# Spreading the last gates of an input phase over the first steps of the output phase, in a fused attention and expert kernel

## Chip, cores and metric

The kernel runs on one core of one Trainium2 chip. The metric is the device time of one execution in microseconds. Engines are named as in the profile: PE is TensorE (PEld its weight loads), DVE is VectorE, ACT is ScalarE, POOL is GpSimd, SP the queue that issues the DMAs.

## What is computed

The reference cut to its core: an attention with a local and a global window, then two expert layers on 3072 tokens.

```python
x = attention(q, k, v)                   # 3072 x 512 after the heads are joined
a, b = x @ w1, x @ w2                    # 512 -> 1024
x2 = ((a * b) @ w3) @ w_out              # first layer, 1024 -> 1024 -> 512
h = x2 @ w_in                            # second layer, 512 -> 2048
g = h * np.cos(h)                        # the gate
out = g @ w_out2                         # 2048 -> 512
```

## The kernel before

Float32 matmuls run as three passes over values that are split into a high half (a cast to fp32r) and a low half (value minus high half): high x high, high x low, low x high (`mm3`, line 419). So every activation that goes into TensorE needs a cast on ScalarE and a subtraction on VectorE ahead of it. A step's first matmul needs only the high half of its activation, the second the low half.

Attention and the first expert layer end at about 615 us of the span. The stage behind it is the second layer, which the change touches. It does its two matrix products by a scheme of seven products in place of eight, with sums and differences of quarter blocks formed before and after. The tokens come in three groups q of two times 512. For each q there are two phases:

- **Input phase A** (`phase_a(q, k, ...)`, k = 0 to 7): one round k makes seven products of six matmuls of 512 columns (`prod`) into PSUM banks; VectorE adds them into two pairs of tiles, jj (gate `g0[k]`) and gg, named gr in the profile (gate `g1[k]`), each 128 x 1024. A gate then computes h times cos(h): `turns` on ScalarE (line 1090, an integer tile in PSUM), two argument operations on VectorE (`rest_steps`, line 1099, which read that PSUM tile), `size` and `cosine` on ScalarE (lines 1105 and 1108) and the product `times` (line 1113) on GpSimd. The gates of round k are finished during rounds k + 1 and k + 2; `fold` (line 1236) then takes a difference of two gated blocks, in A on GpSimd.
- **Output phase B** (`phase_b(q)`): 56 steps in the order of the list `turn`. Step `at` takes block (i, k) of product i and does six matmuls. The first 14 steps are blocks (0, 0) to (0, 6) and (3, 0) to (3, 6), then (2, 0) to (2, 6), then the three blocks with k = 7, then four products of eight blocks. `op_split` makes the two halves of a block into a tile "op": a cast on ScalarE (line 1218) and a subtraction on VectorE (line 1219). It runs four steps ahead of its step. The first four (low halves 0 to 3 in what follows) are made in or right behind the last rounds of A, two of them on GpSimd.

When A ends, gates are left over: the product of `g0[6]`, and all of `g1[7]` and `g0[7]` but one `turns`. `last_gates` is a generator that issues them; a `yield` in it ends what one step of B issues. In the kernel before it issues them in three blocks, at steps 0, 1 and 3, ahead of the split of the same step, with the products on GpSimd.

The order of work on each engine is the order in which the code is written (`manual_schedule`): an engine takes its instructions in that order and waits at one whose operands are not there. Tiles come from rings. "op" tiles alternate between two buffers of their own and four of the tag "Wb", by the counter `op_count` modulo 6; the arguments r of the gates take the same four "Wb" buffers, those of the last two gates take two buffers "x2f", into which later the inputs of the next group (`x2_loads`, `x2_steps`) go. `x2_steps` is also a generator: 18 pieces of work on ScalarE and VectorE that prepare the activations of the next group; a part runs in B, the rest in round 0 of the next A. `pieces_to` issues the weight loads on SP's queue ahead of their use. `evict` takes finished PSUM banks out in B.

```python
for i, (l_hi, l_lo, r_hi, r_lo) in enumerate(terms):
    for e, (l, r) in enumerate(((l_hi, r_hi), (l_hi, r_lo), (l_lo, r_hi))):
        nc.tensor.matmul(ps, lhsT=l, rhs=r, ...)
```

Of the kernel before, what the change touches and what calls it, by code (L numbers as in the profile page):

```python
# [13 lines left out]
ALU = mybir.AluOpType  # L14
# [23 lines left out]
NP = M2 // 2  # L38
# [233 lines left out]
def fused(ctx, tc, a_qk, a_v, a_v0, w3p, wo1p, w1p, w2p, winp, wo2p, out):  # L272
    nc = tc.nc
# [476 lines left out]
    with tc.manual_schedule():  # L750
# [234 lines left out]
        def some(steps, n):  # L985
            for _ in range(n):
                next(steps, None)
# [95 lines left out]
        class Gate:  # L1083
# [25 lines left out]
                    self.r, self.r, ACTF.Sin, scale=-1.0, bias=half_pi[:, 0:1]  # L1109
                )  # L1110

            def times(self):
                nc.gpsimd.tensor_tensor(out=self.h, in0=self.r, in1=self.h, op=ALU.mult)  # L1113

        turn = []
        for prods, ks in (
# [24 lines left out]
        g0, g1 = {}, {}  # L1141

        def phase_a(q, k, x2_last):

            pieces_to(2 * q * (NP * 7 // 2) + (7 * k + 13) // 2)
            jj = wts.tile([128, 2, TB2], F32, tag="wB", name="jj")
            gg = p2.tile([128, 2, TB2], F32, tag="gr", name="gr", bufs=8)
            g0[k], g1[k] = Gate(jj), Gate(gg)
            sv = misc.tile([128, 2, TB2], F32, tag="raw", name="sv", bufs=3)
            vv = misc.tile([128, 2, TB2], F32, tag="raw", name="vv", bufs=3)  # L1150
            s1, s, v = sv[:, 0, :], sv[:, 1, :], vv[:, 0, :]

            def add(out, p, q):
                nc.vector.tensor_tensor(out=out, in0=p, in1=q, op=ALU.add)

            def gate(g, at, what, *args):
                if at >= 0:
                    getattr(g[at], what)(*args)

            prod(q, k, 0)  # L1160
            prod(q, k, 1)
            gate(g1, k - 1, "rest")
            gate(g0, k - 2, "cosine")
            nc.scalar.copy(out=s1, in_=banks["a"])
            gate(g0, k - 2, "times")
            gate(g0, k - 1, "turns")
            add(s, banks["b"], s1)
            gate(g1, k - 1, "size")
            gate(g1, k - 1, "cosine")
            gate(g1, k - 1, "times")  # L1170
            if k:
                fold(3, k - 1, nc.gpsimd)
            if k > 1:
                fold(2, k - 2, nc.gpsimd)
            if k >= NP - 2:
                op_split(0, k - NP + 2, nc.gpsimd)
            prod(q, k, 2)
            prod(q, k, 3)
            some(x2_last, 2)
            add(v, banks["c"], s)  # L1180
            if k:
                steps = g0[k - 1].rest_steps()
                next(steps)
            add(gg[:, 1, :], banks["d"], v)
            if k:
                next(steps)
            some(x2_last, 2)
            prod(q, k, 4)
            prod(q, k, 5)
            run(x2_last)  # L1190
            prod(q, k, 6)
            nc.scalar.copy(out=jj[:, 0, :], in_=banks["a"])
            gate(g0, k - 1, "size")
            add(gg[:, 0, :], banks["c"], s)
            g1[k].turns()
            add(jj[:, 1, :], banks["d"], s)
            if k == NP - 1:
                op_split(0, 2)
                op_split(0, 3)

        t3 = {}

# [7 lines left out]
        ops, op_count = {}, [0]  # L1210
# [27 lines left out]
        def last_gates():  # L1238

            k = NP - 1  # L1240
            homes = [
                late.tile([128, 2, TB2], F32, tag="x2f", name="r", bufs=2) for _ in range(2)
            ]
            a, b = g1[k].rest_steps(homes[0]), g0[k].rest_steps(homes[1])
            next(a)
            next(a)
            g0[k - 1].cosine()
            g0[k - 1].times()
            yield
            g0[k].turns()  # L1250
            g1[k].size()
            g1[k].cosine()
            g1[k].times()
            yield
            yield
            next(b)
            next(b)
            g0[k].size()
            g0[k].cosine()
            g0[k].times()  # L1260
            yield

        def phase_b(q):

            final = q == NQ - 1
# [3 lines left out]
            x2_next = None  # L1269
# [66 lines left out]

            for at, (n, k) in enumerate(turn):
                pieces_to(base + pairs_of.index((n, k // 2)) + 6)
                some(gates, 1)
                if at + 4 < len(turn):  # L1340
                    op_split(*turn[at + 4])
                if at in (8, 10, 12):
                    fold(*{8: (2, NP - 2), 10: (3, NP - 1), 12: (2, NP - 1)}[at])
                if at == 8 and not final:
                    x2_loads(q + 1)
                    r0, r1 = (
                        late.tile([128, 2, TB2], F32, tag="x2f", name="x2f", bufs=2)
                        for _ in range(2)
                    )
                    nc.sync.dma_start(out=r0, in_=x2_cols("B12", q + 1))  # L1350
                    x2_next = x2_steps(r0, r1)
                for i, lag in ((1, 21), (6, 31)):
                    if 0 <= at - lag < NP:
                        fold(i, at - lag)
                if x2_next and at >= 16 and at % 3 == 0:
                    some(x2_next, 1)
                if q == 0 and at in (34, 38, 42):
                    flags_of[0] = next(steps_f)
# [106 lines left out]
```

## Time and profile before

| | us |
|---|---|
| median of 3 runs (lowest to highest) | 1122.69 (1121.36 to 1123.53) |
| the profiled execution, its own time | 1121.77 |
| its span in the trace | 1120.0 |
| TensorE busy | 1085.7 |
| VectorE busy | 848.0 |
| ScalarE busy | 730.7 |
| GpSimd busy | 251.2 |
| second expert layer, first to last matmul | 615.35 to 1114.1 |

A window row gives the stretch, its length, then for each engine the busy time and the number of instructions, the granted TensorE clock (1.00 is 2.4 GHz, 0.50 is 1.2 GHz), the share of the DMA engines and GB/s. A timeline row gives the start, the duration, engine, line, operation, output and inputs, and in brackets how long the engine had been idle and what ended that. A row of waits gives who waited for whom, the total, how often and the longest. Busy TensorE is not TensorE at its peak: at half the clock it is busy for twice as long with the same matmuls.

### The profile page before, as it was taken

How to read it: one execution, taken by the hardware profiler on the slowest of the kernel's cores; microseconds unless marked ns; L12 is line 12 of the kernel's file. 1: busy time of each engine (PE TensorE's matmuls, PEld its weight loads, DVE VectorE, ACT ScalarE, POOL GpSimd, SP SyncE). 2: the span in 40 equal slices, each digit the busy share in tenths (PEclk: the TensorE clock that was granted, in tenths of full speed). 3: DMA queues.
4: the chain of work that ended last, by engine and by line, in shares of the span. 5: the costliest groups of instructions: out<-in, count | busy, mean ns of one | idle time of the engine just before them, and what ended most of it. 6: DMA issues, size and time to landing. Idle time of an engine off the chain costs nothing.

```text
span 1120.0 us, 17799 instructions
## 1 busy us (share of the span) xinstructions
PE 1085.7 (97%) x5922; PEld 936.3 (84%) x5922; DVE 848.0 (76%) x1815; ACT 730.7 (65%) x1481; POOL 251.2 (22%) x252
## 2 busy tenths in 40 slices
PE   8999999999999999999999999899999799999897
PEld 5547899999999999999999887587887588887686
DVE  8887677878787876878633688688788697887684
ACT  8988767767767766767523677454578454678452
POOL 0000011111111111111100377100377100377100
PEclk9999999999999999999999999799999899999899
DMA  9854456676667656665360655466655565655362
GB/s 333 284 185 163 153 191 207 208 224 200 220 201 233 210 184 222 212 221 192 114 220 22 216 195 179 168 210 222 225 189 187 171 219 220 233 190 182 105 222 97
DMA packets 88308, 219.24 MB, mean 196 GB/s; under 512 B 9488, under 2 KB 26384, under 8 KB 88208
## 3 DMA queue, kind: packets, MB, share of 16 engines
q1 hardware_dynamic: 87696, 217.44, 58.1%
q8 instruction: 49, 0.80, 0.3%
q10 hardware_dynamic: 512, 0.58, 0.2%
q14 instruction: 51, 0.42, 0.1%
HBM read 176.04 MB, written 41.94 MB: 195 GB/s over the span
## 4 chain that ended last, share of the span: by engine, by line
PE 50%; DVE 7%; ACT 2%; issue 1%; POOL 0%; DVEq 0%; POOLq 0%
PE h_ps L419 29%; PE mm L419 12%; PE k_ps L419 6%; DVE op L1219 3%; DVE r L1099 1%; PE x_ps L644 1%; DVE jj L1236 1%; ACT r L1105 1%; ACT op L1218 1%; PE pt_ps L617 0%; DVE res L1278 0%; ACT r L1108 0%; PE s_ps L559 0%; PE s_ps L555 0%; PE pt_ps L619 0%
## 5 line engine op out<-in xcount | busy, mean ns | idle before, releaser
L610 POOL TENSOR_SCALAR e<-e,st 128x232 f32<-128x232 f32 x148 | 76.1, 525 | 477.0 <-DVE st L602 386.5
L419 PE MATMUL h_ps<-op,piece 128*128 128x512 f32 x576 | 148.8, 416 | 21.7 <-DVE op L1219 13.2
L419 PEld LDWEIGHTS h_ps<-op,piece 128*128 128x128 f32 x576 | 115.0, 202 | 53.6 <-DVE op L1219 16.3
L419 PE MATMUL mm<-xT,wA 128*128 128x384 f32 x768 | 146.8, 340 | 0.5 <-ACT xT L658 0.4
L419 PE MATMUL mm<-ab,W 128*128 128x384 f32 x768 | 146.2, 340 | 0.0
L419 PE MATMUL mm<-xT,wB 128*128 128x384 f32 x768 | 146.2, 339 | 0.0
L419 PE MATMUL h_ps<-T,piece 128*128 128x512 f32 x576 | 138.4, 389 | 0.0
L419 PEld LDWEIGHTS mm<-xT,wA 128*128 128x128 f32 x768 | 130.9, 188 | 3.2 <-issue 1.8
L419 PEld LDWEIGHTS mm<-ab,W 128*128 128x128 f32 x768 | 131.1, 188 | 2.4 <-issue 2.4
L419 PEld LDWEIGHTS mm<-xT,wB 128*128 128x128 f32 x768 | 130.9, 188 | 2.1 <-issue 2.1
L419 PEld LDWEIGHTS h_ps<-T,piece 128*128 128x128 f32 x576 | 108.1, 188 | 22.5
L1113 POOL TENSOR_TENSOR gr<-r,gr 128x1024 f32<-128x1024 f32 x24 | 57.5, 2397 | 285.1 <-ACT r L1108 283.6
L419 PE MATMUL h_ps<-B,piece 128*128 128x512 f32 x432 | 106.3, 390 | 0.7 <-DVE B L948 0.7
L419 PE MATMUL k_ps<-op,piece 128*128 128x512 f32 x432 | 100.5, 390 | 1.2 <-DVE op L1219 1.2
L419 PEld LDWEIGHTS k_ps<-op,piece 128*128 128x128 f32 x432 | 80.8, 188 | 18.9 <-DVE op L1219 2.0
L419 PEld LDWEIGHTS h_ps<-B,piece 128*128 128x128 f32 x432 | 80.9, 188 | 18.1 <-DVE B L948 1.5
L589 ACT ACTIVATE e<-e,top 128x232 f32<-128x232 f32 (+1 forms) x192 | 89.3, 467 | 2.1 <-DVE top L578 2.1
L522 ACT CAST hh<-qk 128x720 fp32r<-128x720 f32 x74 | 58.9, 796 | 46.0 <-PE s_ps L559 42.0
L578 DVE CUSTOM_DVE_ANT_0 e<-s_ps,bias 128x232 f32<-128x232 f32 (+1 forms) x192 | 64.9, 374 | 13.6 <-PE s_ps L559 8.1
L1105 ACT ACTIVATE r<-r 128x1024 f32<-128x1024 f32 x48 | 51.0, 1062 | 35.1 <-DVE r L1099 35.1
L1218 ACT CAST op<-gr 128x512 fp32r<-128x512 f32 x72 | 44.0, 623 | 43.4 <-PE k_ps L419 15.0
L1219 DVE TENSOR_TENSOR op<-jj,op 128x512 fp32r<-128x512 f32 x66 | 54.6, 849 | 17.5 <-ACT op L1218 17.5
(136 smaller groups left out, 1992.0 us busy)
## 6 DMA issues: line engine op xcount, KB each, us to landing
piece<-a_s SPq DMA_DIRECT2D x84, 512.0 KB, 3.3
piece<-o2s SPq DMA_DIRECT2D x84, 512.0 KB, 4.1
qk<-in_a_qk SPq DMA_DIRECT2D x74, 360.0 KB, 3.3
a_s<-ap SPq DMA_DIRECT2D x56, 256.0 KB, 2.4
o2s<-ap SPq DMA_DIRECT2D x56, 256.0 KB, 2.4
v<-in_a_v SPq DMA_DIRECT2D x95, 128.0 KB, 3.3
raw<-in_w3p SPq DMA_DIRECT2D x16, 512.0 KB, 4.9
raw<-in_winp SPq DMA_DIRECT2D x16, 512.0 KB, 3.6
```

Source lines behind the costliest of these rows:

```text
L419: nc.tensor.matmul(ps, lhsT=l, rhs=r, start=first and i + e == 0, stop=last and i == n - 1 and e == 2, skip_group_check=more,)
L522: nc.scalar.copy(out=hh[n], in_=qk_raw[n])
L578: nc.vector.tensor_tensor_reduce(out=es[n][:, e, :w], in0=sp[:, e, :w], in1=bias[:, 2 * p + e, :], scale=-0.125, scalar=3.0e38, op0=ALU.ad ...
L589: nc.scalar.activation(es[n][:, e, :w], es[n][:, e, :w], ACTF.Exp, bias=top[:, n, e:e + 1], scale=-1.0, accum_out=sts[n][:, 0, e:e + 1],)
L610: nc.gpsimd.tensor_scalar(x, x, st[:, 1, e:e + 1], 1.0, ALU.mult, ALU.mult)
L644: nc.tensor.matmul(x[e * 64:(e + 1) * 64, i * 128:(i + 1) * 128], lhsT=vt[:kk, c, e * 64:(e + 1) * 64], rhs=pt[:kk, e, c, :], start=c == 0 ...
L1099: nc.vector.scalar_tensor_tensor(out=self.r, in0=self.kt, scalar=-c, in1=x, op0=ALU.mult, op1=ALU.add)
L1105: nc.scalar.activation(self.r, self.r, ACTF.Abs)
L1113: nc.gpsimd.tensor_tensor(out=self.h, in0=self.r, in1=self.h, op=ALU.mult)
L1218: nc.scalar.copy(out=t[:, 0, :], in_=x)
L1219: engine.tensor_tensor(out=t[:, 1, :], in0=x, in1=t[:, 0, :].bitcast(F32), op=ALU.subtract)
L1236: engine.tensor_tensor(out=out, in0=p, in1=q, op=ALU.subtract)
```

## The change

`times` takes an engine. In the last round of A, GpSimd makes the low halves of steps 2 and 3 and does so ahead of its two folds; the halves of steps 0 and 1 are made one round earlier (rounds 5 and 6). The counter of the op ring is set to zero at the start of each A. `last_gates` is written in 13 pieces instead of four, its three products go to VectorE, and the three last folds on VectorE are part of it. In B a step now issues its split first and its piece of the gates after it. The loads of the next group's inputs go from step 8 to step 14, and their preparation from every third step from 18 on to every second step from 28 on. Two series of folds in B shift by one step.

```diff
--- before.py
+++ after.py
@@ -1109,8 +1109,8 @@
                     self.r, self.r, ACTF.Sin, scale=-1.0, bias=half_pi[:, 0:1]
                 )
 
-            def times(self):
-                nc.gpsimd.tensor_tensor(out=self.h, in0=self.r, in1=self.h, op=ALU.mult)
+            def times(self, engine=nc.gpsimd):
+                engine.tensor_tensor(out=self.h, in0=self.r, in1=self.h, op=ALU.mult)
 
         turn = []
         for prods, ks in (
@@ -1168,12 +1168,17 @@
             gate(g1, k - 1, "size")
             gate(g1, k - 1, "cosine")
             gate(g1, k - 1, "times")
+            if k == NP - 1:
+                op_split(0, 2, nc.gpsimd)
+                op_split(0, 3, nc.gpsimd)
             if k:
                 fold(3, k - 1, nc.gpsimd)
             if k > 1:
                 fold(2, k - 2, nc.gpsimd)
-            if k >= NP - 2:
-                op_split(0, k - NP + 2, nc.gpsimd)
+            if k == 0:
+                op_count[0] = 0
+            if NP - 3 <= k < NP - 1:
+                op_split(0, k - NP + 3, nc.gpsimd)
             prod(q, k, 2)
             prod(q, k, 3)
             some(x2_last, 2)
@@ -1194,9 +1199,6 @@
             add(gg[:, 0, :], banks["c"], s)
             g1[k].turns()
             add(jj[:, 1, :], banks["d"], s)
-            if k == NP - 1:
-                op_split(0, 2)
-                op_split(0, 3)
 
         t3 = {}
 
@@ -1242,22 +1244,34 @@
                 late.tile([128, 2, TB2], F32, tag="x2f", name="r", bufs=2) for _ in range(2)
             ]
             a, b = g1[k].rest_steps(homes[0]), g0[k].rest_steps(homes[1])
+            g0[k - 1].cosine()
+            g0[k - 1].times(nc.vector)
+            g0[k].turns()
             next(a)
+            yield
             next(a)
-            g0[k - 1].cosine()
-            g0[k - 1].times()
-            yield
-            g0[k].turns()
+            yield
+            yield
             g1[k].size()
             g1[k].cosine()
-            g1[k].times()
-            yield
-            yield
             next(b)
+            yield
             next(b)
+            yield
             g0[k].size()
             g0[k].cosine()
-            g0[k].times()
+            g1[k].times(nc.vector)
+            yield
+            yield
+            yield
+            g0[k].times(nc.vector)
+            yield
+            yield
+            fold(2, k - 1)
+            yield
+            fold(3, k)
+            yield
+            fold(2, k)
             yield
 
         def phase_b(q):
@@ -1336,12 +1350,10 @@
 
             for at, (n, k) in enumerate(turn):
                 pieces_to(base + pairs_of.index((n, k // 2)) + 6)
-                some(gates, 1)
                 if at + 4 < len(turn):
                     op_split(*turn[at + 4])
-                if at in (8, 10, 12):
-                    fold(*{8: (2, NP - 2), 10: (3, NP - 1), 12: (2, NP - 1)}[at])
-                if at == 8 and not final:
+                some(gates, 1)
+                if at == 14 and not final:
                     x2_loads(q + 1)
                     r0, r1 = (
                         late.tile([128, 2, TB2], F32, tag="x2f", name="x2f", bufs=2)
@@ -1349,10 +1361,10 @@
                     )
                     nc.sync.dma_start(out=r0, in_=x2_cols("B12", q + 1))
                     x2_next = x2_steps(r0, r1)
-                for i, lag in ((1, 21), (6, 31)):
+                for i, lag in ((1, 20), (6, 32)):
                     if 0 <= at - lag < NP:
                         fold(i, at - lag)
-                if x2_next and at >= 16 and at % 3 == 0:
+                if x2_next and at >= 28 and at % 2 == 0:
                     some(x2_next, 1)
                 if q == 0 and at in (34, 38, 42):
                     flags_of[0] = next(steps_f)
```

The order of the instructions shows it at three places. On VectorE (DVE), at the end of A and in the first steps of B of the first group; L1219, now L1221, is the low half of a split, L1099 an argument operation, L1113 the product of a gate (jj is `g0`, gr is `g1`), t a fold's result. Before:

```order
L1219 TENSOR_TENSOR op<-jj,op 128x512 x2
L1099 SCALAR_TENSOR_TENSOR r<-k_ps,gr 128x1024
L1099 SCALAR_TENSOR_TENSOR r<-k_ps,r 128x1024
L1219 TENSOR_TENSOR op<-jj,op 128x512 x3
L1099 SCALAR_TENSOR_TENSOR r<-k_ps,jj 128x1024
L1099 SCALAR_TENSOR_TENSOR r<-k_ps,r 128x1024
L1219 TENSOR_TENSOR op<-t_7666,op 128x512 x2
```

and now:

```order
L1221 TENSOR_TENSOR op<-jj,op 128x512
L1113 TENSOR_TENSOR jj<-r,jj 128x1024
L1099 SCALAR_TENSOR_TENSOR r<-k_ps,gr 128x1024
L1221 TENSOR_TENSOR op<-jj,op 128x512
L1099 SCALAR_TENSOR_TENSOR r<-k_ps,r 128x1024
L1221 TENSOR_TENSOR op<-jj,op 128x512
L1221 TENSOR_TENSOR op<-t_7666,op 128x512
L1099 SCALAR_TENSOR_TENSOR r<-k_ps,jj 128x1024
L1221 TENSOR_TENSOR op<-t_7666,op 128x512
L1099 SCALAR_TENSOR_TENSOR r<-k_ps,r 128x1024
L1221 TENSOR_TENSOR op<-t_7830,op 128x512
L1113 TENSOR_TENSOR gr<-r,gr 128x1024
```

Two low halves are gone ahead of the first argument operation. The four argument operations stand one by one between low halves, and two of the three products of gates are seen among them.

On GpSimd (POOL), in the last round of A of the first group and behind it. Before, with the three products of the last gates at the end:

```order
L1113 TENSOR_TENSOR jj<-r,jj 128x1024
L1113 TENSOR_TENSOR gr<-r,gr 128x1024
L1236 TENSOR_TENSOR t_8163<-gr 128x512
L1236 TENSOR_TENSOR gr<-gr,jj 128x512
L1219 TENSOR_TENSOR op<-jj,op 128x512
L1113 TENSOR_TENSOR jj<-r,jj 128x1024
L1113 TENSOR_TENSOR gr<-r,gr 128x1024
L1113 TENSOR_TENSOR jj<-r,jj 128x1024
```

and now, from the same product of `g0[5]` on:

```order
L1113 TENSOR_TENSOR jj<-r,jj 128x1024
L1113 TENSOR_TENSOR gr<-r,gr 128x1024
L1221 TENSOR_TENSOR op<-jj,op 128x512 x2
L1238 TENSOR_TENSOR t_8172<-gr 128x512
L1238 TENSOR_TENSOR gr<-gr,jj 128x512
```

Two low halves stand between the last product and the two folds (L1236, now L1238), and nothing follows.

On ScalarE (ACT), at the end of A and in the first steps of B; L1218, now L1220, is the cast of a split, L1090 `turns`, L1105 `size`, L1108 `cosine`. Before:

```order
L1218 CAST op<-jj 128x512 x2
L1108 ACTIVATE r<-r,half_pi 128x1024
L1218 CAST op<-jj 128x512
L1090 ACTIVATE k_ps<-jj 128x1024
L1105 ACTIVATE r<-r 128x1024
L1108 ACTIVATE r<-r,half_pi 128x1024
L1218 CAST op<-jj 128x512 x2
L1105 ACTIVATE r<-r 128x1024
L1108 ACTIVATE r<-r,half_pi 128x1024
L1218 CAST op<-t_7666 128x512 x2
```

and now:

```order
L1090 ACTIVATE k_ps<-gr 128x1024
L1220 CAST op<-jj 128x512
L1108 ACTIVATE r<-r,half_pi 128x1024
L1090 ACTIVATE k_ps<-jj 128x1024
L1220 CAST op<-jj 128x512 x2
L1220 CAST op<-t_7666 128x512
L1105 ACTIVATE r<-r 128x1024
L1108 ACTIVATE r<-r,half_pi 128x1024
L1220 CAST op<-t_7666 128x512
L1220 CAST op<-t_7830 128x512
L1105 ACTIVATE r<-r 128x1024
L1108 ACTIVATE r<-r,half_pi 128x1024
```

Casts stand between the `size` and `cosine` pairs of the gates. The first `size` of a last gate now comes behind the casts of steps 4 to 7, before it came behind that of step 4 alone.

## Rows read from the trace of the kernel before

**Rows 1.** Page: busy time of each engine; granted clock in 40 slices of the span.
```profile
PE 1085.7 (97%) x5922; PEld 936.3 (84%) x5922; DVE 848.0 (76%) x1815; ACT 730.7 (65%) x1481; POOL 251.2 (22%) x252
PEclk9999999999999999999999999799999899999899
```

**Rows 2.** Windows, the phases A, B, A, B, A, B of the second layer.
```profile
615.35:691.50 76.15, 76.15 (x337) 63.05 (x337) 58.99 (x68) 55.97 (x63) 47.84 (x27) 1.00 0.60 202
691.50:783.68 92.18, 83.74 (x339) 65.75 (x339) 74.41 (x103) 45.72 (x70) 9.69 (x6) 0.93 0.56 194
783.68:860.90 77.22, 76.89 (x339) 63.38 (x338) 62.39 (x73) 55.66 (x62) 48.34 (x27) 1.00 0.61 205
860.90:949.55 88.65, 81.37 (x336) 65.11 (x334) 70.66 (x93) 45.33 (x70) 9.29 (x5) 0.94 0.59 202
949.55:1026.40 76.85, 76.52 (x338) 63.07 (x337) 62.24 (x72) 55.28 (x62) 47.72 (x26) 1.00 0.62 205
1026.40:1114.10 87.70, 80.52 (x337) 64.47 (x335) 62.62 (x87) 41.15 (x65) 10.60 (x6) 0.96 0.44 148
```

**Rows 3.** Waits of PE in the second layer: total us, times, longest.
```profile
PE h_ps L419 <- DVE op L1219: 13.2, 8, 2.0
PE h_ps L419 <- ACT op L1218: 5.5, 6, 1.6
PE k_ps L419 <- DVE op L1219: 1.2, 2, 0.9
PE h_ps L419 <- DVE B L948: 0.7, 2, 0.3
```

**Rows 4.** Windows of 5 us in the first B phase.
```profile
700.00:705.00 5.00, 1.92 (x6) 1.05 (x6) 2.78 (x3) 3.02 (x4) 2.35 (x1) 0.92 0.29 101
705.00:710.00 5.00, 4.94 (x11) 3.47 (x11) 2.96 (x4) 1.93 (x2) 0.00 (x0) 0.50 0.29 84
```

**Rows 5.** Timeline of all engines at the first change from A to B.
```profile
687.73 2.40 POOL L1113 TENSOR_TENSOR gr<-r,gr 128x1024 f32<-128x1024 f32 x1 [0.86 <-ACT r L1108]
691.55 1.75 PE L419 MATMUL h_ps<-op,piece 128*128 128x512 f32 x7
692.08 1.12 ACT L1218 CAST op<-jj 128x512 fp32r<-128x512 f32 x2
692.72 1.83 DVE L1219 TENSOR_TENSOR op<-jj,op 128x512 fp32r<-128x512 f32 x1 [0.27 <-ACT op L1218]
692.73 1.27 POOL L1219 TENSOR_TENSOR op<-jj,op 128x512 fp32r<-128x512 f32 x1
694.33 2.48 POOL L1113 TENSOR_TENSOR jj<-r,jj 128x1024 f32<-128x1024 f32 x1 [0.33 <-ACT r L1108]
694.47 2.89 DVE L1219 TENSOR_TENSOR op<-jj,op 128x512 fp32r<-128x512 f32 x1
699.79 1.06 ACT L1105 ACTIVATE r<-r 128x1024 f32<-128x1024 f32 x1 [4.10 <-DVE r L1099]
705.06 1.22 PE L419 MATMUL h_ps<-op,piece 128*128 128x512 f32 x2 [1.98 <-DVE op L1219]
```

**Rows 6.** Groups by shape in the second layer: busy us, mean ns of one.
```profile
L1236 POOL TENSOR_TENSOR t<-gr 128x512 f32<-128x512 f32 x21 | 27.3, 1299 | 1.6
L1105 ACT ACTIVATE r<-r 128x1024 f32<-128x1024 f32 x48 | 51.0, 1062 | 35.1 <-DVE r L1099 35.1
L1108 ACT ACTIVATE r<-r,half_pi 128x1024 f32<-128x1024 f32 x48 | 55.0, 1146 | 0.9
L1099 DVE SCALAR_TENSOR_TENSOR r<-k_ps,r 128x1024 f32<-128x1024 int32 x48 | 58.5, 1219 | 0.9
```

**Rows 7.** Timeline of DVE in the middle of the first B phase.
```profile
744.85 0.68 DVE L1236 TENSOR_TENSOR gr<-gr 128x512 f32<-128x512 f32 x1
745.45 1.22 DVE L948 TENSOR_TENSOR B<-B 128x1024 fp32r<-128x1024 f32 x1
746.59 0.68 DVE L1219 TENSOR_TENSOR op<-gr,op 128x512 fp32r<-128x512 f32 x1
```

More of the change, by code (lines that the diff above doesn't have):

```diff
@@ L1244, in last_gates @@
             a, b = g1[k].rest_steps(homes[0]), g0[k].rest_steps(homes[1])
+            g0[k - 1].cosine()
+            g0[k - 1].times(nc.vector)
+            g0[k].turns()
             next(a)
+            yield
             next(a)
-            g0[k - 1].cosine()
-            g0[k - 1].times()
             yield
-            g0[k].turns()
+            yield
             g1[k].size()
             g1[k].cosine()
-            g1[k].times()
+            next(b)
+            yield
+            next(b)
+            yield
+            g0[k].size()
+            g0[k].cosine()
+            g1[k].times(nc.vector)
             yield
             yield
[L1256 to L1259, printed above, removed]
-            g0[k].times()
+            yield
[7 more added lines that the diff above has]
+            fold(2, k)
             yield
```

## Prediction

> **What bounds the kernel now.** I read the page first: TensorE is busy for 97% of the span, so only what holds TensorE counts, and its clock row dips three times [rows 1]. Next comes the second expert layer cut into its six phases [rows 2]. The input phases (A) and output phases (B) hold 336 matmuls each. The first A takes 76.15 us at a granted clock of 1.00, which is 0.2266 us a matmul and 1.36 us for one step of B (six matmuls). The three B phases take 92.18, 88.65 and 87.70 us for as many matmuls: 16.03 + 12.50 + 11.55 = **40.08 us more than the work needs**. The waits of TensorE name the cause: nearly all are for "op", the high and low halves that a split makes, from VectorE and from ScalarE [rows 3]. The reader is to see in the fine windows that in B's first 20 us TensorE is busy for 1.92 of 5 us, and that its clock then stands at 0.50, which is 1.2 GHz [rows 4].
>
> The timeline shows how it comes about [rows 5]. VectorE's low half of step 2 takes 1.83 us, and that of step 3 takes 2.89 us, where an undisturbed one takes 0.68 [rows 7]. They end 0.55 us after a GpSimd instruction that ran beside them (at 694.00 and 696.81). VectorE's two argument operations of the last gate wait behind them, ScalarE waits 4.10 us for these arguments with the casts of the next splits behind it in its queue, and so TensorE waits another 1.98 us for the low half of step 5. The loop repeats with the second gate. It is a chain GpSimd, VectorE, ScalarE, VectorE, TensorE, and no engine in it is full.
>
> **What the change does, by its own places.**
>
> Removed: the three products of the last gates on GpSimd (2.4 us each, one of them in [rows 5]) no longer run beside splits. Two low halves (steps 2 and 3) leave VectorE for GpSimd and are made during A.
>
> Added on VectorE: three products of 1024 columns, 1.14 us each in a full queue, against two halves of 0.60 saved [rows 7]: 3.4 - 1.2 = +2.2 us per B.
>
> Moved: the two gates lie over steps 0 to 8 instead of in blocks ahead of a split. The folds go one or two steps later or earlier, and the first is not needed before the last block's split. The four x2 loads go on SP's queue from step 8 to step 14, behind four more piece loads; their first reader is now at step 28, 19 us later, so I cost that at nothing (cover: those 14 steps). The x2 operations start at step 28, every second step, where they started at 18, every third. ScalarE gets its casts of steps 2 and 3 a little earlier, beside TensorE's last products of A: nothing. In A the GpSimd work of one round rises to two products, two folds and a half, about 4.8 + 2.6 + 1.3 = 8.7 us, under the 9.52 us of a round (42 x 0.2266): nothing. That the reset of the counter puts steps 0 and 1 always into the same two buffers costs nothing either: buffers of older arguments are free by then.
>
> **The first 13 steps, in order.** Step n's first matmul needs only the high half, so the low half is due at 691.55 + 1.36 n + 0.23; the start of step 0 is a row [rows 5].
> - GpSimd ends the product before the last at 690.13 [rows 5], makes halves 2 and 3 (1.30 each, the length of an instruction of that size [rows 6]) by 692.75, and folds until 694.05 and then once more. Steps 0 to 3 start without a wait; in the trace step 1 waited for GpSimd.
> - Half 4 is cast at 692.08, where now half 2 is cast [rows 5], and reaches VectorE at 692.7. The fold holds it until 694.05; with the 0.55 of the trace it ends at 694.6 (due 697.2).
> - The product of gate g0[6] meets the second fold, 694.6 to 695.9, and ends at 697.0.
> - First argument operation 1.22 [rows 6], half 5, second argument operation: 698.2, 698.8, 700.0.
> - ScalarE: size 1.06 and cosine 1.15 [rows 6], casts of 8 and 9 at 0.56 each: 702.2, then 702.8 and 703.4. VectorE meanwhile makes halves 6 and 7 and the first argument of the other gate, then half 8 at 703.4 and the second argument at 704.6.
> - ScalarE: size, cosine, cast of 10: 707.4; VectorE's half 10 ends at 708.1. Due: 705.4. **Late by 2.7 us**; with some six hand-overs between engines of 0.04 to 0.06 I take 3.0. Behind it the remaining halves and the last product (1.14) fit into their steps: half 13 at 711.2, due at 712.4 + the delay.
>
> At this place a row decides: VectorE is held for 1.3 us twice, 2.6 us of the 3.0, if it waits as the two long halves of [rows 5] did. The Trainium skill (SBUF — State Buffer, "SBUF: two separate sides") says the same more strictly: the port pair of VectorE and GpSimd is an exclusive lock for a whole instruction, also for a VectorE operation with two SBUF inputs. By that rule the change puts new GpSimd work, two halves and then the folds, in front of the first splits, and the 2.6 us stay; if the pair could be shared, the delay would be near 0.4 us. The long halves agree with the rule, and the sum keeps 3.0.
>
> Bounds per phase: 0.4 (no hold) to 4.5 (the product is held by one more instruction of 1.3 us). I keep 3.0, since the rows show the hold each time. Three phases: **9.0 us**, ends 1.2 and 13.5.
>
> **The later steps.** VectorE works there without a gap [rows 7], and TensorE waits once in the first two B phases, 0.9 and 0.3 us [rows 3]. From step 28 to 39 VectorE needs 12 halves (7.2), 8 folds (4.8) and four totals at the block's end (1.14 x 2 + 0.6 x 2 = 3.5). Of x2 operations two fell there (2.3), now four (4.6): 2.3 us more, part of which the four steps of lead take. I put 1.3 us on each of the two phases (ends 0 and 2.3): late waits of 3.8 instead of 1.2 us. In return one x2 operation less is left for the next A, whose wait for B21's low half, 0.33 us twice [rows 3], should go: -0.7.
>
> **Sum.** 40.08 now; 9.0 + 3.8 remain, less 0.7 in A: 40.1 - 12.8 + 0.7 = 28.0 us gained. This counts the clock as whole, since no wait is then longer than about 1.5 us. The profiled execution took 1121.77 us (span 1120.0), so I forecast 1121.8 - 28.0 = **1093.8 us, said as 1094**. The median of the runs shown is 0.9 us above the profiled one, within the range.
>
> Ends of the unknown costs: 1.2 + 1.2 left gives 37.0 to 38.4 us gained, about 1084; 13.5 + 5.8 left gives 20.8, about 1101.
>
> **Rivals.**
> 1. **The clock falls all the same.** In the trace it fell behind waits of up to 1.98 us [rows 5], in a stretch with TensorE busy for 1.92 of 5 us [rows 4]. The delay of 3 us, spread over steps 5 to 10, may be enough. Eleven matmuls run in 5 us at 0.50 against 22 at full clock, so each such stretch costs 2.5 us; two stretches in each of three phases are 15 us, one is 7.5: 1101 to 1109. Against it: more than half of TensorE's time is then busy. The Trainium skill (TensorE: Matmul & The Clock Gate, "A second HAM failure mode: psum-queue depth-cycling") says that short idle times between groups of matmuls can make the clock go up and down; in the late waits of this trace, 0.9 us at most, it stayed at 1.00.
> 2. **Slower: the splits lose their lead.** ScalarE and VectorE work strictly in order, the gates now stand between the splits, and the cast of step 5 writes a buffer that TensorE's step 2 reads. If the lead at step 4 is gone, every step from 4 to 13 pays cast and half in series, 0.62 + 0.68 = 1.3, or 13 us, plus three products and four arguments, 3.4 + 4.9 = 8.3: 21 us in each phase, 64 in place of 38.9 at the gates: about 1147. It decides from a half 4 later than 697.2. Against it: half 4 is ready 2.6 us before that.
> 3. **Nothing moves.** The work of the gates is the same and one place waits for the other, as if VectorE were the bound: three products more, and the time stays at 1122. Against it: VectorE needs 13 halves (7.8), four arguments (4.9), three products (3.4) and 2.6 of holds, 18.7 us, in 17.7 us of steps; it is over by 1 us and not by 13.
> 4. **Better still:** VectorE isn't held, late waits don't grow: below 1088.
>
> **How the numbers follow.** Forecast 0.73 (1088 to 1101), rival 1 0.16 (1101 to 1109), rival 4 0.05, rival 2 0.04, rival 3 0.02. The range 1088 to 1105 takes the forecast and half of rival 1. A difference of 0.2% (2.2 us) is about what a measurement of this kernel can tell from none; so faster 0.94, same 0.02, slower 0.04.
>
> **What would show it.** In the changed profile the B phases should last about 79 to 81 us, the clock row should have no dips after the attention, and the long waits for "op" should be gone. VectorE's half 4 and the product of g0[6] should be stretched to about 1.8 and 2.4 us, and those at later steps not. TensorE should wait around steps 5 to 10, last for a cast that stands behind a cosine, and once near step 40. The prediction is wrong if B lasts over 85 us, if the clock falls, or if TensorE waits 1 us or more before step 4.

## The result and the profile after

The changed kernel takes 1093.02 us (median of 4 runs, 1092.42 to 1093.30) against 1123.01 us before (1121.36 to 1123.53): a ratio of 0.9735, 95% interval 0.9718 to 0.9752. Forecast were 1094, with 1088 to 1105 as the range. The profiled execution took 1093.30 us, 28.47 us less than the profiled one before; the sum of the prediction was 28.0.

The page of the changed kernel, busy time and granted clock:

```profile
PE 1073.5 (98%) x5922; PEld 928.7 (85%) x5922; DVE 842.7 (77%) x1818; ACT 729.7 (67%) x1481; POOL 237.8 (22%) x249
PEclk9999999999999999999999999999999999999999
```

VectorE and GpSimd are busy for less than in [rows 1], though VectorE got more instructions, and no digit of the clock row is below 9 any more (it is a mean over 27 us; a short dip is shown below). The six phases, with the columns of [rows 2]:

```profile
614.89:691.09 76.20, 76.20 (x338) 63.08 (x337) 59.00 (x68) 57.06 (x65) 49.27 (x28) 1.00 0.64 202
691.09:773.96 82.87, 79.95 (x339) 63.74 (x338) 72.59 (x105) 44.12 (x68) 4.06 (x3) 0.98 0.61 217
773.96:850.12 76.16, 76.16 (x337) 63.06 (x336) 61.03 (x71) 56.26 (x64) 49.25 (x28) 1.00 0.62 207
850.12:930.61 80.49, 78.19 (x338) 62.52 (x336) 71.11 (x95) 43.93 (x68) 4.07 (x3) 1.00 0.63 222
930.61:1006.77 76.16, 76.16 (x338) 63.08 (x336) 61.03 (x71) 56.25 (x64) 49.28 (x28) 1.00 0.62 207
1006.77:1085.50 78.73, 77.59 (x337) 62.50 (x335) 61.52 (x87) 40.00 (x63) 4.06 (x3) 1.00 0.49 165
```

The output phases last 82.87, 80.49 and 78.73 us in place of 92.18, 88.65 and 87.70 [rows 2]. The second and third input phase, 77.22 and 76.85 before, are now as long as the first. So the three output phases together are 26.4 us shorter. TensorE's idle time in them fell from 22.9 to 6.4 us, 16.5 of it; the other 9.9 us are busy time of the same matmuls, whose granted clock is 0.98 to 1.00 in place of 0.93 to 0.96. What TensorE still waits for, to be held against [rows 3]:

```profile
PE k_ps L419 <- DVE op L1221: 2.9, 2, 1.8
PE h_ps L419 <- ACT op L1220: 2.3, 3, 0.8
PE h_ps L419 <- DVE op L1221: 0.7, 3, 0.2
```

Waits of 13.2 + 5.5 us for halves into the bank h_ps have become 0.7 + 2.3; those into k_ps, which belong to the later steps, have grown from 1.2 to 2.9. The wait for B is gone. One kind of wait of the kernel before is missing in [rows 3], that for the low half of step 1, which GpSimd makes there behind its two folds:

```profile
PE h_ps L419 <- POOL op L1219: 3.0, 3, 1.4
```

It is gone too: GpSimd now makes that half a round earlier. The first steps of the first output phase, as the timeline has them (GpSimd, VectorE, ScalarE, TensorE):

```profile
689.63 2.57 POOL L1221 TENSOR_TENSOR op<-jj,op 128x512 fp32r<-128x512 f32 x2
692.13 1.32 POOL L1238 TENSOR_TENSOR t<-gr 128x512 f32<-128x512 f32 x1
693.39 1.76 POOL L1238 TENSOR_TENSOR gr<-gr,jj 128x512 f32<-128x512 f32 x1
692.25 1.74 DVE L1221 TENSOR_TENSOR op<-jj,op 128x512 fp32r<-128x512 f32 x1 [0.27 <-ACT op L1220]
693.92 2.31 DVE L1113 TENSOR_TENSOR jj<-r,jj 128x1024 f32<-128x1024 f32 x1
695.42 0.62 ACT L1220 CAST op<-jj 128x512 fp32r<-128x512 f32 x1 [1.23 <-PE h_ps L419]
704.87 1.15 ACT L1108 ACTIVATE r<-r,half_pi 128x1024 f32<-128x1024 f32 x1
705.93 2.16 ACT L1220 CAST op<-t 128x512 fp32r<-128x512 f32 x4
691.09 14.74 PE L419 MATMUL h_ps<-op,piece 128*128 128x512 f32 x60
706.58 0.50 PE L419 MATMUL h_ps<-op,piece 128*128 128x512 f32 x1 [0.75 <-ACT op L1220]
707.31 5.08 PE L419 MATMUL h_ps<-op,piece 128*128 128x512 f32 x21 [0.22 <-DVE op L1221]
```

These answer to [rows 5]. Step 0 starts at 691.09, 0.46 us earlier than before; the layer itself starts that much earlier (614.89 for 615.35), which has nothing to do with the change. Half 4 on VectorE is held by the first fold (1.74 us for 0.68), the first product by the second fold (2.31 for 1.22). The second fold is itself held: 1.76 us in place of 1.30. ScalarE's cast of step 5 waits 1.23 us for TensorE's step 2, whose buffer it takes. The last cast before step 10 stands behind the second cosine, and there TensorE waits visibly, 0.75 + 0.22 us. The 60 matmuls ahead of it took 14.74 us where 13.6 are needed; that is lateness in pieces too small to show as idle time. The second matmul of step 10 starts at 707.31, where 691.09 + 61 x 0.2266 = 704.91 was due: **2.4 us late**.

Near step 40 of the same phase (TensorE, VectorE, and the window):

```profile
751.09 3.25 PE L419 MATMUL k_ps<-op,piece 128*128 128x512 f32 x13
756.11 6.22 PE L419 MATMUL k_ps<-op,piece 128*128 128x512 f32 x19 [1.78 <-DVE op L1221]
751.80 1.21 DVE L1292 TENSOR_TENSOR sum<-k_ps,sum 128x1024 f32<-128x1024 f32 x1
752.93 1.20 DVE L1292 TENSOR_TENSOR res<-k_ps,res 128x1024 f32<-128x1024 f32 x1
754.17 1.29 DVE L1292 TENSOR_TENSOR res<-h_ps,res 128x512 f32<-128x512 f32 x2
755.38 0.68 DVE L1221 TENSOR_TENSOR op<-gr,op 128x512 fp32r<-128x512 f32 x1
755.00:760.00 5.00, 3.89 (x11) 3.03 (x12) 4.92 (x10) 2.77 (x5) 0.00 (x0) 0.69 0.72 229
```

Four totals of the finished blocks, 3.6 us in a row, come between two low halves on VectorE. TensorE waits 1.78 us, and in the window behind that its clock is at 0.69 in the mean, so partly at 1.2 GHz: 19 matmuls fill 6.22 us. In the second output phase the same wait is 1.12 us, and 23 matmuls behind it take 5.87 us at full clock. The dip doesn't belong to the wait as such. In the run with the two folds on VectorE the wait is as long, the clock in that window is 1.00, and 23 matmuls behind it take 5.88 us, where the same 23 take 7.13 us here:

```profile
754.95 5.88 PE L419 MATMUL k_ps<-op,piece 128*128 128x512 f32 x23 [1.78 <-DVE op L1221]
```

Four more of the runs below have this wait with 1.77 or 1.78 us and a clock of 1.00 behind it (the spread alone, the halves on VectorE, the gates' piece ahead, the last cosine later); one dips as the changed kernel does (the products back on GpSimd, 23 matmuls in 7.15 us). In the kernel before, the two late waits were 0.92 and 0.26 us, so each has grown by 0.86. That the first is 0.66 us longer, then as now, goes with work on flags that only the first output phase has: two operations of 0.27 us on VectorE (lines 737 and 739) stand right ahead of the low half in front of the totals. No run leaves them out.

### The profile page after: what moved, and what is told of

The parts are those of the page before. It is cut to its first block, busy times and chain, and to the rows that moved or that the text cites. A ratio compares the mean times of both kernels' runs of the same rounds, so it can differ in the third digit from the quotient of the medians.

```text
span 1091.4 us, 17792 instructions
## 1 busy us (share of the span) xinstructions
PE 1073.5 (98%) x5922; PEld 928.7 (85%) x5922; DVE 842.7 (77%) x1818; ACT 729.7 (67%) x1481; POOL 237.8 (22%) x249
## 4 chain that ended last, share of the span: by engine, by line
PE 50%; DVE 6%; ACT 2%; issue 1%; POOL 0%; DVEq 0%; ACTq 0%; POOLq 0%
PE h_ps L419 29%; PE mm L419 13%; PE k_ps L419 6%; DVE op L1221 2%; DVE r L1099 1%; PE x_ps L644 1%; DVE jj L1238 1%; ACT op L1220 1%; DVE jj L1113 1%; ACT r L1105 1%; DVE res L1292 0%; PE pt_ps L617 0%; PE s_ps L559 0%; PE s_ps L555 0%; PE pt_ps L619 0%
## 5 line engine op out<-in xcount | busy, mean ns | idle before, releaser
L610 POOL TENSOR_SCALAR e<-e,st 128x232 f32<-128x232 f32 x148 | 76.2, 527 | 476.4 <-DVE st L602 366.9
L419 PE MATMUL h_ps<-op,piece 128*128 128x512 f32 x576 | 136.7, 393 | 3.4 <-ACT op L1220 2.3
L419 PEld LDWEIGHTS h_ps<-op,piece 128*128 128x128 f32 x576 | 107.0, 188 | 31.2 <-DVE op L1221 6.1
L1113 POOL TENSOR_TENSOR gr<-r,gr 128x1024 f32<-128x1024 f32 x21 | 50.6, 2408 | 285.2 <-ACT r L1108 283.8
L1220 ACT CAST op<-gr 128x512 fp32r<-128x512 f32 x72 | 43.6, 622 | 34.0 <-PE k_ps L419 16.2
L1105 ACT ACTIVATE r<-r 128x1024 f32<-128x1024 f32 x48 | 51.0, 1062 | 21.9 <-DVE r L1099 21.9
L869 PE MATMUL mm<-wo,w 128*128 128x512 f32 x128 | 61.2, 606 | 1.8 <-DVE wo L360 1.8
```

The lines of the kernel that those rows point to most:

```text
L419: nc.tensor.matmul(ps, lhsT=l, rhs=r, start=first and i + e == 0, stop=last and i == n - 1 and e == 2, skip_group_check=more,)
L610: nc.gpsimd.tensor_scalar(x, x, st[:, 1, e:e + 1], 1.0, ALU.mult, ALU.mult)
L869: nc.tensor.matmul(W_ps[m], lhsT=wt["w3", c][:, m * 128:(m + 1) * 128], rhs=wt["wo1", k], start=k == 0, stop=k == M1 - 1,)
L1105: nc.scalar.activation(self.r, self.r, ACTF.Abs)
L1113: engine.tensor_tensor(out=self.h, in0=self.r, in1=self.h, op=ALU.mult)
L1220: nc.scalar.copy(out=t[:, 0, :], in_=x)
```

## The experiments

The theory: VectorE's low halves were held by GpSimd's products, the gates stood in blocks ahead of the splits, and both had to go. The first rival: the spread is what counts. The second: the engine of the products is all. Ratios are to the kernel before on the same chip, with 95% intervals; the changed kernel's own is 0.9735.

### Products back on GpSimd

```diff
-            g0[k - 1].times(nc.vector)
+            g0[k - 1].times()
...
-            g1[k].times(nc.vector)
+            g1[k].times()
...
-            g0[k].times(nc.vector)
+            g0[k].times()
```

> The changed kernel with the three products of the last gates back on GpSimd, at the places in the order that they now have. Theory (GpSimd's products hold VectorE's low halves, and so the engine counts): each product runs 2.4 us on GpSimd beside low halves on VectorE and holds one of them for up to that time, and its own result comes 1.2 us later; about half of the gain goes: 1103 to 1109 us, output phases of 84 to 88 us, low halves of 1.5 to 3 us beside the products. Rival (the spread over 13 steps is what counts, the engine hardly): 1092 to 1096 us.

Measured: 1109.95 us, 0.9896 (0.9877 to 0.9916), a little above the theory's interval and far from the rival's. The timeline (ScalarE, GpSimd, VectorE, TensorE):

```profile
697.28 1.14 ACT L1220 CAST op<-jj 128x512 fp32r<-128x512 f32 x2 [3.37 <-POOL jj L1113]
694.84 2.41 POOL L1113 TENSOR_TENSOR jj<-r,jj 128x1024 f32<-128x1024 f32 x1
702.11 2.37 POOL L1113 TENSOR_TENSOR gr<-r,gr 128x1024 f32<-128x1024 f32 x1 [4.87 <-DVE r L1099]
702.58 2.45 DVE L1221 TENSOR_TENSOR op<-t,op 128x512 fp32r<-128x512 f32 x1 [0.49 <-ACT op L1220]
705.09 3.16 PE L419 MATMUL h_ps<-op,piece 128*128 128x512 f32 x11 [1.65 <-DVE op L1221]
711.48 4.87 PE L419 MATMUL h_ps<-op,piece 128*128 128x512 f32 x20 [1.98 <-DVE op L1221]
```

A low half takes 2.45 us beside GpSimd's second product, much like those in [rows 5]. There is a second price, larger than was expected: the casts of steps 5 and 6 wait 3.37 us for the first product's end. GpSimd comes to this product behind its two folds and then needs 2.41 us for it, so that it ends at 697.25, 6.4 us into the output phase; in the changed kernel it ends 5.1 us into it, though it is held there, and the wait for it is 0.22 us.

### The kernel before, with the products alone on VectorE

```diff
-            def times(self):
-                nc.gpsimd.tensor_tensor(out=self.h, in0=self.r, in1=self.h, op=ALU.mult)
+            def times(self, engine=nc.gpsimd):
+                engine.tensor_tensor(out=self.h, in0=self.r, in1=self.h, op=ALU.mult)
...
-            g0[k - 1].times()
+            g0[k - 1].times(nc.vector)
...
-            g1[k].times()
+            g1[k].times(nc.vector)
...
-            g0[k].times()
+            g0[k].times(nc.vector)
```

> The kernel before with one part of the change alone: the three products of the last gates on VectorE, still in blocks ahead of the splits at steps 0, 1 and 3. Theory (the holds by GpSimd cost about as much as the blocks): 1103 to 1109 us, about half of the gain. Rival (the spread counts): over 1115 us. Rival (the products' engine is all): under 1097 us.

Measured: 1112.23 us, 0.9912 (0.9892 to 0.9932): a third of the gain, between the theory and the first rival, so that neither came in; the second rival is out. No half is held by a product now, but the blocks stay; ScalarE and TensorE at the second gate:

```profile
704.01 1.06 ACT L1105 ACTIVATE r<-r 128x1024 f32<-128x1024 f32 x1 [3.86 <-DVE r L1099]
706.15 3.21 ACT L1218 CAST op<-t 128x512 fp32r<-128x512 f32 x6
706.80 0.79 PE L419 MATMUL h_ps<-op,piece 128*128 128x512 f32 x1 [2.98 <-ACT op L1218]
```

ScalarE waits 3.86 us for the last arguments with the casts of the next six steps behind it, and TensorE waits 2.98 us for the first of those. This is the part that the spread removes.

### The spread alone

```diff
             if k == NP - 1:
-                op_split(0, 2, nc.gpsimd)
-                op_split(0, 3, nc.gpsimd)
...
             add(jj[:, 1, :], banks["d"], s)
+            if k == NP - 1:
+                op_split(0, 2)
+                op_split(0, 3)
...
-            g0[k - 1].times(nc.vector)
+            g0[k - 1].times()
...
-            g1[k].times(nc.vector)
+            g1[k].times()
...
-            g0[k].times(nc.vector)
+            g0[k].times()
```

> The changed kernel with the products on GpSimd and the low halves of steps 2 and 3 on VectorE at the end of the input phase, as before; what stays is the order of the last gates' pieces behind the splits, the later folds and the later preparation of the next group. Theory: 1101 to 1109 us, since the holds by GpSimd stay. Rival (the spread counts, the engine doesn't): 1092 to 1097 us.

Measured: 1105.01 us, 0.9862 (0.9838 to 0.9886), half of the gain, as the theory has it. The first experiment, which differs by the two low halves on GpSimd, comes out 0.3% slower, with intervals that just overlap. The casts of steps 5 and 6 wait 1.60 us for GpSimd's product here, against 3.37 there, which fits two instructions fewer ahead of the product on GpSimd. Besides what the expectation lists, this run keeps the halves of steps 0 and 1 a round earlier on GpSimd.

### Low halves of steps 2 and 3 on VectorE

```diff
             if k == NP - 1:
-                op_split(0, 2, nc.gpsimd)
-                op_split(0, 3, nc.gpsimd)
...
             add(jj[:, 1, :], banks["d"], s)
+            if k == NP - 1:
+                op_split(0, 2)
+                op_split(0, 3)
```

> The changed kernel with the low halves of steps 2 and 3 made by VectorE at the end of the input phase, as before, and the halves of steps 0 and 1 one round earlier on GpSimd, as now. Theory (what GpSimd does behind the last product of the input phase holds VectorE's first operations, so two instructions fewer there make up for two more on VectorE): 1089 to 1093 us, the same or up to 3 us faster. Rival (the four halves on GpSimd are the lead that the gates live on): 1 to 2 us slower in each output phase, 1096 to 1099 us.

Measured: 1091.22 us, 0.9728 (0.9710 to 0.9745): the same as the changed kernel within the intervals, and the rival with 1096 us or more is out. The halves of steps 2 and 3 on GpSimd are no part of the gain. Those of steps 0 and 1 are not tested: they stay a round earlier here and in the run before, and no run undoes that. TensorE's waits for GpSimd's half, 3.0 us in the kernel before and 1.5 with the products alone on VectorE, are gone in every run that has it, so its share counts here as part of the spread.

In thousandths of the time before, the spread alone gives 13.8, the products alone 8.8, both together 27.2 (this run), and the low halves of steps 2 and 3 on GpSimd nothing on top (26.5). Both together give 4.6 more than the two single gains added up; each figure is uncertain by about 2, so that is little more than the noise, and why it is so stays open.

### The two folds behind them on VectorE

```diff
-            if k:
+            if 0 < k < NP - 1:
                 fold(3, k - 1, nc.gpsimd)
-            if k > 1:
+            if 1 < k < NP - 1:
                 fold(2, k - 2, nc.gpsimd)
...
+            fold(3, k - 1)
             g0[k].times(nc.vector)
             yield
             yield
+            fold(2, k - 2)
+            yield
             fold(2, k - 1)
```

> The changed kernel with the two folds of the last round of the input phase moved from GpSimd to VectorE, to steps 8 and 10 of the output phase. It takes away what runs on GpSimd beside VectorE's half 4 and first product, and adds 2 x 0.6 us to VectorE at later steps. Theory (the holds are most of the delay in the first steps): half 4 takes 0.7 us and the first product 1.2 us instead of 1.74 and 2.31, and each output phase gets 1 to 2.5 us shorter: 1086 to 1090 us. Rival (the delay comes from cast and cosine on ScalarE alone): 1092.5 to 1095 us, since VectorE gets more to do.

Measured: 1088.67 us, 0.9706 (0.9693 to 0.9719). VectorE's half 4 and first product in this run:

```profile
692.30 0.69 DVE L1221 TENSOR_TENSOR op<-jj,op 128x512 fp32r<-128x512 f32 x1 [0.28 <-ACT op L1220]
693.36 1.23 DVE L1113 TENSOR_TENSOR jj<-r,jj 128x1024 f32<-128x1024 f32 x1 [0.36 <-ACT r L1108]
```

0.69 and 1.23 us in place of 1.74 and 2.31: with nothing on GpSimd they aren't held, and the kernel is 3 us (by the ratios) to 4 us (by the medians) faster, though VectorE does more. So the folds' hold was worth 1.1 to 1.4 us of the 2.4 in each phase. The trace of the first output phase agrees:

```profile
706.16 5.51 PE L419 MATMUL h_ps<-op,piece 128*128 128x512 f32 x23 [0.23 <-DVE op L1221]
```

This is the second matmul of step 10; with step 0 at 691.13 it was due at 704.95, so it is 1.2 us late where it was 2.4.

### Gates' piece ahead of the split

```diff
+                some(gates, 1)
                 if at + 4 < len(turn):
                     op_split(*turn[at + 4])
-                some(gates, 1)
```

> The changed kernel with one line moved: in each step of the output phase the gates' piece is issued ahead of that step's split again. Theory (what counts is that the pieces are small and where the products run, not which of the two is first): 1091 to 1095 us. Rival (behind the splits is what makes it): 1 us or more later in each output phase, 1096 us or more.

Measured: 1092.33 us, 0.9732 (0.9718 to 0.9745), no difference. With the pieces as small as they are here, behind or ahead of the split doesn't matter. The timeline of GpSimd and VectorE has a by-product:

```profile
692.88 1.33 POOL L1238 TENSOR_TENSOR t<-gr 128x512 f32<-128x512 f32 x1
694.14 2.30 POOL L1238 TENSOR_TENSOR gr<-gr,jj 128x512 f32<-128x512 f32 x1
693.54 1.75 DVE L1113 TENSOR_TENSOR jj<-r,jj 128x1024 f32<-128x1024 f32 x1 [0.81 <-ACT r L1108]
```

The first product of the gates comes first here and is held by the first fold; the second fold then takes 2.30 us for 1.30, held by VectorE.

### Other places for the later work

```diff
-                if at == 14 and not final:
+                if at == 12 and not final:
...
-                for i, lag in ((1, 20), (6, 32)):
+                for i, lag in ((1, 20), (6, 40)):
...
-                if x2_next and at >= 28 and at % 2 == 0:
+                if x2_next and at >= 20 and at % 3 == 0:
```

> The changed kernel with other places for the later work alone: the folds of product 6 at steps 40 to 47 instead of 32 to 39, the next group's loads at step 12 and its preparation at every third step from 20 (21) on. Theory (VectorE is over-full between steps 28 and 40, which costs 4.1 us in the first output phase and 1.8 in the second, above the 2.5 us of the third): 1.5 to 4 us faster, 1089 to 1091.5 us, with the wait of 1.8 us near step 40 gone; against that 0.3 us may come back in the next input phase. Rival (the wait near step 40 comes from the totals at the end of a block, whatever else stands there): 1092 to 1094 us.

Measured: 1090.19 us, 0.9713 (0.9700 to 0.9726). TensorE's waits:

```profile
PE h_ps L419 <- ACT op L1220: 2.3, 3, 0.8
PE h_ps L419 <- DVE op L1221: 0.7, 3, 0.2
PE h_ps L419 <- DVE B L948: 0.7, 2, 0.3
```

The waits into k_ps, 2.9 us, are gone with the totals in their place, so it was the load around them. The run moves three things at once; the next one, which moves the loads and the preparation alone, takes only 0.5 of the 2.9 us away, which leaves most to the folds. The interval still overlaps with the changed kernel's, but the trace has the gain where it should be: the first two output phases last 79.28 and 78.72 us in place of 82.87 and 80.49, and the third, which has no preparation, is as long as it was. The wait for B in the input phase is back, 0.7 us, as expected.

### Preparation of the next group as before

```diff
-                if at == 14 and not final:
+                if at == 8 and not final:
...
-                if x2_next and at >= 28 and at % 2 == 0:
+                if x2_next and at >= 16 and at % 3 == 0:
```

> The changed kernel with the loads of the next group at step 8 and its preparation at every third step from 16 on, as in the kernel before. Theory (the later, denser preparation costs VectorE its lead near step 40, and gives back a short wait in the next input phase): 1090.5 to 1092.5 us, the late waits of 1.8 and 1.1 us shorter by about 0.5 us each, and 0.3 us of waits for B21 back in the second and third input phase. Rival (the preparation had to go later, since the gates now fill VectorE up to step 13): 1094 us or more.

Measured: 1092.64 us, 0.9742 (0.9725 to 0.9758): the same as the changed kernel within the intervals, 0.1 us above the theory's range. The late waits were 2.4 instead of 2.9 us and 0.7 us of waits for B came back; the two cancel. The time alone doesn't exclude the rival, but the trace does: TensorE has no wait between the one at step 10 and the late one, so the gates don't need the later start.

### The last cosine one step later

```diff
             next(b)
             yield
-            g0[k].size()
-            g0[k].cosine()
             g1[k].times(nc.vector)
             yield
+            g0[k].size()
+            g0[k].cosine()
             yield
```

> The changed kernel with the size and cosine of the very last gate issued one step later, so that the cast of step 10 stands ahead of them in ScalarE's queue. Theory (what is left of the delay in the first steps is that cast behind the cosine, 0.75 + 0.23 us in each output phase, on top of lateness from the holds): 1 to 1.5 us less per output phase, 1088.5 to 1090.5 us, and no wait of 0.7 us for ScalarE at step 10. Rival (VectorE is late anyway, so the wait goes from ScalarE's cast to VectorE's low half and stays): 1092 to 1093.5 us.

Measured: 1089.56 us, 0.9715 (0.9697 to 0.9733). TensorE's waits in the second layer, all of them:

```profile
PE k_ps L419 <- DVE op L1221: 2.9, 2, 1.8
```

No wait for halves into h_ps is left, so TensorE's wait for ScalarE at step 10 had no second one behind it. That decides against the rival; the time doesn't, since its interval overlaps with the changed kernel's. By the trace the second and third output phase are 1.2 us shorter each (79.29 and 77.67 us).

### All three together

The folds on VectorE, the later work in other places and the last cosine one step later, as in the three diffs above.

> The changed kernel with the folds of the last round of the input phase on VectorE (steps 8 and 10), the later work at the places of the run on the later steps, and the size and cosine of the very last gate one step later, behind the cast of step 10. Theory: the output phases come to within 1 us of the input phases, 76.2 to 77.2 us, so 1081 to 1084 us. Rival (VectorE is full, what is taken from one place comes back in another): 1087 us or more.

Measured: **1082.99 us**, 0.9648 (0.9634 to 0.9661), 10 us below the changed kernel. The output phases (columns as above) and TensorE's waits:

```profile
691.92:768.90 76.98, 76.98 (x339) 62.84 (x338) 70.58 (x106) 43.15 (x67) 1.09 (x1) 1.00 0.64 221
845.69:922.09 76.40, 76.40 (x338) 62.84 (x336) 69.21 (x96) 43.15 (x67) 1.10 (x1) 1.00 0.65 223
998.91:1075.40 76.49, 76.49 (x337) 62.77 (x335) 60.58 (x89) 39.77 (x63) 1.11 (x1) 1.00 0.51 169
```

```profile
PE h_ps L419 <- DVE B L948: 0.7, 2, 0.3
```

They last 76.98, 76.40 and 76.49 us; 76.2 is what the matmuls take. What is left to wait for in this layer is 0.7 us.

## Why the prediction was right, step by step

- **The bound and its price.** 40.08 us of excess in the output phases were there to be won. Now 82.87 + 80.49 + 78.73 - 3 x 76.20 = 13.5 us are left; 12.8 were forecast. The waits for GpSimd's half of step 1, 3.0 us, are part of the 40.08, though they stand neither in [rows 3] nor by themselves in the sum.
- **The first 13 steps.** Forecast 2.7 us late at step 10, taken as 3.0; measured 2.4 in the first phase, and 2.5 as the whole excess of the third, which has no later load. The chain came as written: half 4 held by a fold, the product by the next one, then two rounds of arguments, size, cosine and cast. The hold came out at 1.1 us each (1.74 - 0.68, 2.31 - 1.22), not 1.3. The run with the folds moved shows it is a hold and not VectorE's own load, though it was worth 1.1 to 1.4 us a phase and not the 2.6 that was put down to it: the cast of step 10 behind the cosine stays.
- **The hold itself.** The Trainium skill (SBUF — State Buffer, "SBUF: two separate sides") has the pair of ports as an exclusive lock for whichever of the two engines starts first. The runs agree on both sides: low halves of 1.74 to 2.45 us beside GpSimd, and folds of 1.76 and 2.30 us in place of 1.30 beside VectorE. The second side is missing in the prediction's steps.
- **The later steps: the term that was mis-sized.** The prediction put 1.3 us more on each of the first two phases, 3.8 in all. Measured are 82.87 - 76.20 - 2.5 = 4.2 and 1.8, together 6.0. The waits themselves grew by less than was put, 0.86 us each. The second phase fits; the first has a stretch at half the clock on top, about 1.3 us (7.13 for 5.88 behind the wait) that five of the runs with the same wait don't have. That the load near step 40 was the cause of the waits is shown by the run with other places for it.
- **The input phases.** Forecast 0.7 us, measured 77.22 + 76.85 - 2 x 76.16 = 1.75. Half a microsecond of that is only the edges of the windows in [rows 2]: the second output phase starts at 860.47 and not at 860.90, the third at 1026.33. From first matmul to first matmul both input phases before took 76.8 us, so 1.25 is gained; the wait costs more than its idle time.
- **Rivals.** The clock did fall once, for part of 5 us and not in the first steps but behind the late wait, so rival 1 came in small, and in a place that the prediction had held safe because 0.9 us there had not been enough. The prediction had named a fall of the clock as a sign of being wrong; for this one stretch the sign came true. A half 4 ready at 693.99 was in time, so rival 2 had no chance; its waiting for step 2's buffer was there, 1.23 us, without harm. Rival 3 is out by the result, and rival 4 by the two holds and the late waits; the run with all three edits shows what it would have been worth.
- **What was luck.** The sum (28.0) lies 0.5 us from the profiled gain (28.47) because its errors cancel: the first steps cost about 7.5 us and not 9.0, the later ones 6.0 and not 3.8, the input phases gave 1.25 and not 0.7, and 0.46 us come from the earlier start of the layer. The range didn't need that luck.
- **A judgement that fell.** The prediction counted the two low halves on GpSimd as a part of the change that pays in the first steps. The run without them is as fast: they save VectorE 1.2 us and put 2.6 us of GpSimd in front of its first operations.

## What to carry to other kernels

Where two engines hold each other, read the long durations and not the idle time: here an operation that took 2.9 us where its like takes 0.7 was the wait, and what ended 0.55 us ahead of its end was the cause. A block of dependent work on in-order queues can be cut into small pieces and laid over steps in which the consumer has lead; which piece comes first in a step mattered nothing here. A part of a change can pay nothing by itself, so single parts are worth undoing even when the whole is fast: here three of them paid nothing (two halves on GpSimd, the splits ahead of the gates, the later preparation), and what still held TensorE was worth another 10 us.

## What the runs showed that was not expected

- VectorE holds GpSimd as well: a 128 x 512 fold on GpSimd, 1.30 us alone, took 1.76 us in the changed kernel and 2.30 us with the gates' piece first.
- An argument operation on VectorE, which reads one tile from PSUM and one from SBUF, was not held. GpSimd and VectorE in the run with the products on GpSimd; 1.22 us is the mean of such operations in [rows 6]:

```profile
693.12 1.77 POOL L1238 TENSOR_TENSOR gr<-gr,jj 128x512 f32<-128x512 f32 x1
693.65 1.21 DVE L1099 SCALAR_TENSOR_TENSOR r<-k_ps,gr 128x1024 f32<-128x1024 int32 x1
```

- The clock followed single waits loosely. With the spread alone TensorE was busy for 3.34 and 2.19 us in two windows of 5 us at 1.00, and the clock was lower only in the third:

```profile
701.00:706.00 5.00, 3.34 (x15) 2.32 (x13) 4.52 (x4) 1.86 (x4) 2.38 (x1) 1.00 0.21 85
706.00:711.00 5.00, 2.19 (x8) 1.05 (x6) 2.78 (x3) 4.97 (x8) 2.36 (x1) 1.00 0.33 105
711.00:716.00 5.00, 5.00 (x15) 3.98 (x16) 5.00 (x9) 1.31 (x3) 0.00 (x0) 0.66 0.31 105
```

In the kernel before, a window with 1.92 us had 0.92 already, and the next 0.50 [rows 4]. The same wait of 1.78 us near step 40 was followed by 0.69 in the changed kernel and by 1.00 in the run with the folds on VectorE. What makes the difference stays open.
